# Hash-bucketed attention and a GELU feed-forward on one core: the requests for W_in move to ScalarE's queue, and four orders in the first and last pairs of heads change

## The chip, the core and the metric

The kernel runs on one core of a Trainium2 chip, in one launch. The metric is the device time of one execution in microseconds (us). Of the kernel before, three runs are given; of each kernel one execution was also recorded by the hardware profiler, and the profile and the trace are of that execution.

The names used: PE is TensorE (the matrix engine), DVE is VectorE, ACT is ScalarE, POOL is GpSimd, SP is SyncE, which here does nothing but issue DMAs. SPq and ACTq are the DMA issues in the instruction streams of SP and ACT. PSUM is the memory that the matmuls write.

## The reference, cut to what matters

q, k and v are of shape (4, 8, 768, 64): 4 batches, 8 heads, 768 positions, 64 dimensions, in fp32. `proj` is 64 x 6.

```
q_bits, k_bits = (q @ proj > 0), (k @ proj > 0)          # 6 bits a position
mask   = bucket(q_bits)[:, None] == bucket(k_bits)[None, :]
scores = where(mask, q @ k.T / 8, -1e9)
attn   = softmax(scores) @ v                              # (4, 8, 768, 64)
x      = attn.transpose(0, 2, 1, 3).reshape(3072, 512)
h      = x @ w_in                                         # 512 -> 2048
out    = (h * sigmoid(1.702 * h)) @ w_out                 # 2048 -> 512
```

Every position attends only to the positions in the same hash bucket. `w_in` and `w_out` arrive as 64-bit floats and are turned into 32-bit ones on the chip.

## The kernel before, in words

**Stages.** `attention` (L289 to L736) takes the 32 heads in 16 pairs, n = 0 to 15; the two heads of a pair share the 128 partitions. `feed_forward` follows with a nest of products of halves and quarters (a Strassen-like scheme that needs sums of quarters of x, W_in and W_out). The attention builds x in `xT` (features on partitions, 3072 positions on the free axis) and, pair by pair, turns one 128 x 512 chunk of W_in from 64 to 32 bits.

**One pair.** For each pair n:

- `fetch(n, "k")` and `fetch(n, "q")` (L342, DMAs at L353, four each) and `fetch_v` (L355, DMAs at L365, two) bring the pair's inputs, one to three pairs ahead. `turn` (L414) transposes k and q on DVE into a tile `own` (three in turn; in the profile they also carry the name s_in, whose room one of them uses). `exchange` (L419, four DMAs `s_in<-own` at L424) writes a second copy with the halves of 32 rows swapped.
- `measure` (L426) sums the squares of k or q on ACT into a column of `sizes`; its elementwise output is not used ("junk"). At the end `guard` (L584) takes the largest of the sums, and decides whether a slower, shifted attention must run instead.
- `hashed` (L435) multiplies with `proj` on PE; `featured` (L444) makes the bits into features `f` with one DVE operation (L446), and eight small DMAs (L454) bring f into the tile `feat` of that pair (two in turn). `spread` (L456, two DMAs at L459, then `exchange`) copies the features to further partitions, for pairs from 3 on. A product of features adds 0 to scores of equal buckets and a very large negative number to the others.
- `scores_of_four` (L477) computes four tiles of scores on PE (128 keys x 384 queries of both heads), each with `weigh` (L462): the exponential on ACT (L463). Pairs 0 to 2 use whole rows of 64 (L474), later ones four parts of 32 rows (L491) that run beside each other.
- `values` (L517, matmuls at L524) multiplies the exponentials with v; `unload` (L532) brings the result to `xT` on ACT (L535, L536).
- The denominators: `add_low` (L502 on POOL) and `add_high` (L512, L515 on DVE) add the exponentials over the key tiles, `total` (L538, PE at L546) sums them over the partitions, `invert` (L548, DVE: transpose `rt` at L552, reciprocals at L555 and L559, transpose at L561) inverts, and `norm` (L565, DVE at L567) multiplies `xT` with it. All this happens one or two pairs later.

**The conversion of W_in.** `convert` (L161) is a generator: a DMA brings the raw 512 KB of a chunk (`raw`, L165, one tile), then six DVE operations (L181, L185, L189, L196, L200, L203) and one square on ACT (L193) turn it. `begin(n)` (L576) starts chunk n-2 and issues its DMA; `step(n)` moves a chunk on by one operation. A chunk takes until the beginning of the next pair, where its last operation (L203) frees `raw`.

**PSUM.** Four score tiles s0 to s3 are taken in turn by `in_turn` (L308). The same tiles hold the results of `hashed`, `total` and `values`. A matmul that takes a tile waits until the reader of its last contents is done: the exponential, the unload, the write of f, or the transpose `rt`.

**Sums of x.** `x_sums` (L582) holds four DVE operations on quarters of x (L225 to L228): `x_sums[0]` in pair 14, `x_sums[1]` at the end of pair 14, `x_sums[2]` (L227) in pair 15, `x_sums[3]` (L228) behind the last pair. `in_sums(0)` does the like for W_in on POOL (L217 to L220).

**What sets the order.** The orders of PE, DVE, ACT and POOL are those of the program text (`ORDERED`). SP's order comes from the framework's scheduler. Each DMA is given one of eight completion semaphores in turn, in the scheduler's order over all queues, and so waits for the landing of the DMA eight places before it.

**Around the change, before.** In each pair from 3 on the order is: the write of f for the next pair; `rt` of the pair n-2; the last step of the running chunk; `begin(n)`, which puts the request for the next raw chunk on SP; the feature DMAs on SP; and then the first four tiles of scores. The first chunk, chunk 0, is begun at the end of pair 1. `f` has one buffer. `measure(3, "q")` stands in pair 1, and `fetch(4, "q")` too. `unload(0, 0)` stands behind `featured(1)`, two of whose DMAs go out on ACT's queue. In pair 15 `x_sums[2]` runs on DVE early, and two steps of the last chunk stand ahead of the transpose `rt` of pair 14.

Of the kernel before, what the change touches and what calls it, by code (L numbers as in the profile page):

```python
# [38 lines left out]
def kernel(  # L39
# [249 lines left out]
    def attention(ff):  # L289
# [4 lines left out]
        with actx:  # L294
# [131 lines left out]
            def measure(n, name):  # L426

                x = raws[n, name]
                i = 2 * n + "kq".index(name)
                junk = st.tile([P, S], BF16, tag="junk", name="junk", bufs=1)  # L430
                nc.scalar.activation(junk, x.rearrange("p s i -> p (s i)"), Act.Square, accum_out=sizes[:, i : i + 1])

            dots = {}

            def hashed(n, at):  # L435

                h = dots[n] = at[:, 0:HS]
                for i, x in enumerate("kq"):
                    for c in range(2):
                        r0 = D * i + 32 * c  # L440
                        nc.tensor.matmul(h[r0 : r0 + 32, :], pf[x], xts[n, x][:, c * HS : (c + 1) * HS],
                                         start=True, stop=True)

            def featured(n):  # L444
                f = wk.tile([P, HS], BF16, tag="f", name="f", bufs=1)
                nc.vector.tensor_scalar(f, dots.pop(n), above[:, 0:1], weight[:, 0:1], op0=Alu.is_gt, op1=Alu.mult)  # L446
                yield
                for c in range(2):
                    for i, x in enumerate("kq"):

                        queue = nc.scalar if (n, x, c) == (1, "q", 0) else nc.sync
                        for j in range(2):
                            r0 = D * i + 32 * c + 16 * j
                            queue.dma_start(out=feats[n % 2][x][D * j : D * j + 16, c * HS : (c + 1) * HS], in_=f[r0 : r0 + 16, :])  # L454
# [110 lines left out]
            def norm(n):  # L565
                x, rs = x_of(n), accs.pop(n)
                nc.vector.tensor_tensor(x, x, rs.rearrange("p (t s) -> p t s", t=T), op=Alu.mult)  # L567
# [4 lines left out]
            def step(n, count=1):  # L572
                for _ in range(count):
                    next(conv.get(n, iter(())), None)

            def begin(n):  # L576
                if 0 <= n - 2 < len(in_chunks) - LATE:
                    conv[n] = convert(cv, *in_chunks[n - 2])
                    step(n)


# [29 lines left out]
            measure(1, "q")  # L611
            values(0, 0, high, at[:, 0])
            hashed(1, at[:, 1])
            whole(featured(1))
            unload(0, 0)
            fetch(2, "q")
            fetch_v(1)
            scores(0, 1, high, slots)
# [6 lines left out]
            for n in range(1, last + 1):  # L625

                more = n + 2 <= last
                if n > 1:
                    if n < last:
                        features = featured(n + 1)  # L630
                        next(features)
                    if n > 2:
                        inverse[n - 2] = invert(n - 2)
                        next(inverse[n - 2])
                        step(n - 1)
                        begin(n)
                    if n < last:
                        whole(features)
                scores_of_four(n, ((0, 0), (0, 2)))
                add_high(n - 1, 1, (0, 1))  # L640
                add_low(n, 0)
                if n > 1:
                    next(inverse[n - 2])
                    if more:
                        turn(n + 2, "k")
                    elif n < last:
                        x_sums[0]()
                    else:
                        guard(0)
                        x_sums[2]()  # L650
                add_high(n - 1, 1, (2,))
                if n > 1:
                    norm(n - 2)
                    if more:
                        measure(n + 2, "k")
                    if n + 3 <= last:
                        fetch(n + 3, "k")
                    values(n - 1, 1, every, in_turn()[:, 0])
                    unload(n - 1, 1)
                else:  # L660
                    for x in "kq":
                        turn(2, x)
                    measure(2, "q")
                    for x in "kq":
                        fetch(3, x)
                if n < last:
                    fetch_v(n + 1)
                    if n + 1 >= BY_PARTS:
                        spread(n + 1)
                add_high(n, 0, (0,))  # L670
                step(n, 2)
                scores_of_four(n, ((0, 4), (1, 0)))
                add_low(n, 1, (0,))
                step(n)
                add_high(n, 0, (1,))
                if n > 1 and more:
                    turn(n + 2, "q")
                elif n + 1 == last:
                    x_sums[1]()
                add_high(n, 0, (2,))  # L680
                if more:
                    for x in "kq" if n == 1 else "q":
                        measure(n + 2, x)
                    if n > 1 and n + 3 <= last:
                        fetch(n + 3, "q")
                at = in_turn()
                values(n, 0, every, at[:, 0])
                if n == 1:
                    at1 = in_turn()
                    hashed(2, at[:, 1])  # L690
                    total(0, at1[:, 0])
                if n == last:
                    total(n - 1, at[:, 1])
                unload(n, 0)
                if n == 1:
                    whole(featured(2))
                if n == last:
                    step(n, 2)
                if n in (1, last):
                    inverse[n - 1] = invert(n - 1)  # L700
                    next(inverse[n - 1])
                if n == 1:
                    for x in "kq":
                        turn(3, x)
                        fetch(4, x)
                scores_of_four(n, ((1, 2), (1, 4)))
                add_low(n, 1, (1,))
                if n < last:
                    step(n, 2)
                    at = in_turn()  # L710
                    if more:
                        hashed(n + 2, at[:, 0])
                    if n > 1:
                        total(n - 1, at[:, 1])
                    if n == 1:
                        begin(2)
            next(inverse[last - 1])
            add_high(last, 1, late=True)
            at = place(0)
# [5 lines left out]
            nc.gpsimd.tensor_copy(low_sum[0:1, 0, 0:1], accs_last[0][0:1, 0, 0:1])  # L725
            for f in in_sums(0):
                f()
            norm(last - 1)
            x_sums[3]()
            step(last)  # L730
            inverse = invert(last)
            next(inverse)
# [688 lines left out]
    def whole(steps):  # L1421
        for _ in steps:
            pass
# [49 lines left out]
```

## Time and profile before

| | |
|---|---|
| median of three runs | 865.67 us (864.15 to 866.25) |
| the profiled execution's own time | 865.41 us |
| its span (first to last instruction) | 863.5 us |
| granted clock of TensorE, mean | 0.998 |
| PE, DVE, ACT, POOL busy | 98%, 80%, 39%, 42% of the span |
| pairs 0 and 1, up to 48.09 us | 48.09 us |
| pairs 2 to 15, to 325.23 us | 277.14 us |
| feed-forward, to the end of the span | 538.27 us |

About 1.9 us of the profiled execution's time lie outside its span. How to read the rows: a row of a timeline has the start in us from the span's start, the duration, the engine (SPq and ACTq: a DMA issue), the line of the kernel, the operation, output <- inputs, sizes, a count (xN: N alike in a row, with the time from the first's start to the last's end), and in brackets the idle time of the engine ahead of it and what ended that. A row of a window has its two ends and its length, and then, for PE, the weight loads, DVE, ACT and POOL, the busy time and the number of instructions, and at last the granted clock, the DMA engines' busy share and GB/s. "Pair n" in times means: from PE's first score matmul of that pair to the first of the next one; since the pairs overlap, other pairs' work lies in it too.

### The profile page before, as it was taken

Reading aid. Unit: us, or ns where it says so; the run is one execution under the profiler, and the core shown is the slowest. Engines: PE = TensorE matmul, PEld = TensorE weight load, DVE = VectorE, ACT = ScalarE, POOL = GpSimd, SP = SyncE. Lnnn points to the kernel's source line nnn. Section 1 sums busy time; section 2 is a strip of 40 time slices with the busy share of each in tenths; the row PEclk is TensorE's granted clock in tenths of the full one; section 3 lists DMA queues with packets and bytes.
Section 4 is the critical chain, followed back from the end, with each engine's and each line's share of the span. In section 5 each row is a group of like instructions: output and inputs, shape, how many; then the busy total and the mean of one; then the engine's idle time right before and its main releaser. Section 6 shows DMA issues by size and latency. Waiting matters only on the chain.

```text
span 863.5 us, 15037 instructions
## 1 busy us (share of the span) xinstructions
PE 846.1 (98%) x5631; PEld 524.0 (61%) x5631; DVE 691.7 (80%) x1069; ACT 337.2 (39%) x549; POOL 365.6 (42%) x321
## 2 busy tenths in 40 slices
PE   8999999999999999999999999999999999999996
PEld 4444444444444444566666666644888888888885
DVE  4479788988979995787888888676998977897786
ACT  5666767666656653344444444443000000000000
POOL 4333434333333338999764367568764100000000
PEclk9999999999999999999999999999999999999999
DMA  5648787677767302427465545577854675477534
GB/s 129 104 69 168 147 149 150 130 142 135 130 132 147 84 26 87 158 98 274 165 250 205 202 172 202 212 268 261 277 175 165 201 237 203 155 228 227 194 117 99
DMA packets 165197, 144.04 MB, mean 167 GB/s; under 512 B 124384, under 2 KB 139872, under 8 KB 159872
## 3 DMA queue, kind: packets, MB, share of 16 engines
q1 hardware_dynamic: 156720, 118.76, 50.5%
q10 hardware_dynamic: 8400, 24.28, 8.3%
q8 instruction: 45, 0.74, 0.4%
q14 instruction: 32, 0.26, 0.1%
HBM read 79.69 MB, written 50.33 MB: 151 GB/s over the span
## 4 chain that ended last, share of the span: by engine, by line
PE 80%; DVE 6%; DMA 5%; SPq 3%; issue 2%; ACT 2%; ACTq 0%; DVEq 0%
PE product L1196 29%; PE product L869 22%; PE s L524 9%; PE s L491 7%; PE small L937 6%; PE product L937 3%; DMA raw<-in_moe_w_in_dram 2%; SPq L353 2%; PE s L474 1%; DVE acc L515 1%; ACT e L463 1%; DMA q<-in_q_dram 1%; SPq L454 1%; DVE bits L185 1%; DVE w_in_sb L181 1%
## 5 line engine op out<-in xcount | busy, mean ns | idle before, releaser
L463 ACT ACTIVATE e<-s 128x768 f32<-128x768 f32 x192 | 145.1, 811 | 52.2 <-PE s L491 43.7
L524 PE MATMUL s<-e,v 128*32 128x385 f32 x1536 | 131.1, 488 | 1.0 <-issue 1.0
L502 POOL TENSOR_TENSOR t_x<-e 128x768 f32<-128x768 f32 x32 | 59.3, 1853 | 142.1 <-ACT e L463 117.5
L869 PE MATMUL product<-xT,w_in_sb 128*128 128x512 f32 x216 | 100.0, 593 | 0.1
L524 PEld LDWEIGHTS s<-e,v 128*32 128x32 f32 x1536 | 46.9, 109 | 80.3 <-issue 65.7
L869 PE MATMUL product<-t_x,s_in 128*128 128x512 f32 x192 | 89.4, 592 | 0.0
L491 PE MATMUL s<-s_in 32*128 32x384 f32 x816 | 82.4, 483 | 0.1
L502 POOL TENSOR_TENSOR t_x<-t_x,e 128x768 f32<-128x768 f32 x32 | 55.2, 1726 | 54.2 <-ACT e L463 52.8
L515 DVE TENSOR_TENSOR acc<-acc,e 128x768 f32<-128x768 f32 x63 | 68.6, 1088 | 2.3
L1232 ACT COPY u<-product 128x256 f32<-128x256 f32 x20 | 7.4, 372 | 158.1 <-PE product L1196 124.9
L869 PEld LDWEIGHTS product<-xT,w_in_sb 128*128 128x128 f32 x216 | 40.9, 190 | 35.8 <-issue 32.7
L491 PEld LDWEIGHTS s<-s_in 32*128 32x128 f32 x816 | 42.2, 185 | 21.0 <-issue 1.5
L869 PEld LDWEIGHTS product<-t_x,s_in 128*128 128x128 f32 x192 | 36.5, 190 | 29.7 <-issue 27.0
L491 PE MATMUL s<-own 32*128 32x384 f32 x432 | 46.1, 486 | 0.0
L885 DVE TENSOR_TENSOR u<-product,u 128x256 f32<-128x256 f32 (+1 forms) x60 | 28.4, 486 | 15.9 <-PE product L937 12.8
L491 PE MATMUL s<-feat 32*128 32x384 bf16 x312 | 30.7, 327 | 6.1 <-ACT xT L536 3.2
L491 PEld LDWEIGHTS <-feat 32*128 32x128 bf16 x312 | 9.7, 91 | 42.0 <-issue 28.4
L1196 PE MATMUL product<-raw_g,xT 128*128 128x256 f32 x152 | 35.1, 379 | 0.0
L512 DVE SCALAR_TENSOR_TENSOR acc<-t_x,e 128x768 f32<-128x768 f32 x31 | 29.4, 948 | 5.7 <-ACT e L463 3.6
L226 POOL TENSOR_TENSOR v<-c,v 128x1024 f32<-128x1024 f32 (+1 forms) x15 | 32.4, 2157 | 1.0
L225 POOL TENSOR_TENSOR u<-v,u 128x1024 f32<-128x1024 f32 (+1 forms) x11 | 23.8, 2165 | 21.1 <-ACT v L882 11.9
L885 DVE TENSOR_TENSOR v<-product,v 128x512 f32<-128x512 f32 x24 | 16.5, 689 | 20.2 <-PE product L869 20.2
(298 smaller groups left out, 1813.9 us busy)
## 6 DMA issues: line engine op xcount, KB each, us to landing
raw_g<-g_dram SPq DMA_DIRECT2D x20, 1024.0 KB, 5.1
s_in<-g_dram SPq DMA_DIRECT2D x20, 1024.0 KB, 5.1
g_dram<-c ACTq DMA_DIRECT2D x18, 512.0 KB, 2.9
raw<-in_moe_w_out_dram ACTq DMA_DIRECT2D x16, 512.0 KB, 3.7
raw<-in_moe_w_in_dram SPq DMA_DIRECT2D x15, 512.0 KB, 3.9
s_in<-own SPq DMA_DIRECT2D x36, 192.0 KB, 4.0
v<-in_v_dram SPq DMA_DIRECT2D x32, 192.0 KB, 4.0
k<-in_k_dram SPq DMA_DIRECT2D x60, 96.0 KB, 3.1
```

The costliest lines, as they stand in the source:

```text
L225: return [lambda: eng.tensor_tensor(t1, b12, b11, op=Alu.subtract), lambda: eng.tensor_tensor(b12, b22, b12, op=Alu.subtract), lambda: eng ...
L226: lambda: eng.tensor_tensor(b12, b22, b12, op=Alu.subtract),
L463: nc.scalar.activation(es[c][:, kt, :, 0:HS], ps[:, :, 0:HS], Act.Exp, scale=1.0 / D**0.5)
L491: nc.tensor.matmul(ps[i][:, j, 0:HS], a[r0 : r0 + 32, keys], m[r0 : r0 + 32, cols], start=at == 0, stop=at == 2)
L502: nc.gpsimd.tensor_tensor(low_sum, low_sum if i else e[:, 0], e[:, i + 1], op=Alu.add)
L512: nc.vector.scalar_tensor_tensor(acc, terms[0], T * TINY, terms[1], op0=Alu.add, op1=Alu.add)
L515: nc.vector.tensor_tensor(acc, acc, terms[i + 1], op=Alu.add)
L524: nc.tensor.matmul(av[D * j + d : D * j + d + 32, :], vt[:, t, j, d : d + 32], es[c][:, t, j, :], start=(t == 0), stop=(t == T - 1))
L869: nc.tensor.matmul(ps, wq[LEFT[i]][:, kc, :], xq[RIGHT[i]][:, kc, :], start=(start and kc == 0), stop=(kc == K2 - 1), skip_group_check=not ...
L885: nc.vector.tensor_tensor(dst, x, y, op=Alu.add)
L937: nc.tensor.matmul(x, wq[LEFT[i]], xq[RIGHT[i]], start=start, stop=True, skip_group_check=True)
L1196: nc.tensor.matmul(ps, wq[LEFT[i]][:, c, :], gq[RIGHT[i]][:, c, :], start=(onto is None and c == 0), stop=(c == F4 - 1), skip_group_check= ...
```

## The change

- `measure` writes its unused output as fp32 into the columns of `xT` that belong to the last pair of heads (which are written with x later), in place of a bf16 tile of its own.
- `f` has two buffers in place of one.
- `begin` passes ACT's queue to `convert`: the raw chunk's DMA (L165) is issued by ACT. `begin(n)` stands behind the pair's first four tiles of scores, and so behind their four exponentials on ACT, in place of the start of the pair. For n = 2 it stands in pair 2 in place of the end of pair 1. It is 14 DMAs in all, one in each of the pairs 2 to 15. SP keeps 24 of 25 DMAs a pair.
- In pair 0 `unload(0, 0)` stands ahead of `featured(1)` and its two DMAs on ACT's queue.
- `measure(3, "q")` and `fetch(4, "q")` move from pair 1 into pair 2, behind its first exponentials.
- In pair 15 `x_sums[2]` moves behind the attention, beside `x_sums[3]`, after POOL's sums of W_in and ahead of `norm` of pair 14. The two steps of the last chunk stand behind `rt` of pair 14 in place of ahead of it.

The orders of PE and POOL stay as they were. In the changed program the raw chunk on ACT waits, in the steady pairs, for the landing of the third of the eight feature DMAs of the same pair (eight places before it) and for L203 of the chunk before.

```diff
--- before.py
+++ after.py
@@ -427,8 +427,8 @@
 
                 x = raws[n, name]
                 i = 2 * n + "kq".index(name)
-                junk = st.tile([P, S], BF16, tag="junk", name="junk", bufs=1)
-                nc.scalar.activation(junk, x.rearrange("p s i -> p (s i)"), Act.Square, accum_out=sizes[:, i : i + 1])
+                junk = xT[:, HP - 1, (B - 1) * S : B * S].rearrange("p (s i) -> p s i", i=32)
+                nc.scalar.activation(junk, x, Act.Square, accum_out=sizes[:, i : i + 1])
 
             dots = {}
 
@@ -442,7 +442,7 @@
                                          start=True, stop=True)
 
             def featured(n):
-                f = wk.tile([P, HS], BF16, tag="f", name="f", bufs=1)
+                f = wk.tile([P, HS], BF16, tag="f", name="f", bufs=2)
                 nc.vector.tensor_scalar(f, dots.pop(n), above[:, 0:1], weight[:, 0:1], op0=Alu.is_gt, op1=Alu.mult)
                 yield
                 for c in range(2):
@@ -575,7 +575,7 @@
 
             def begin(n):
                 if 0 <= n - 2 < len(in_chunks) - LATE:
-                    conv[n] = convert(cv, *in_chunks[n - 2])
+                    conv[n] = convert(cv, *in_chunks[n - 2], nc.scalar)
                     step(n)
 
 
@@ -611,8 +611,8 @@
             measure(1, "q")
             values(0, 0, high, at[:, 0])
             hashed(1, at[:, 1])
+            unload(0, 0)
             whole(featured(1))
-            unload(0, 0)
             fetch(2, "q")
             fetch_v(1)
             scores(0, 1, high, slots)
@@ -633,10 +633,13 @@
                         inverse[n - 2] = invert(n - 2)
                         next(inverse[n - 2])
                         step(n - 1)
-                        begin(n)
                     if n < last:
                         whole(features)
                 scores_of_four(n, ((0, 0), (0, 2)))
+                if n == 2:
+                    measure(3, "q")
+                    fetch(4, "q")
+                begin(n)
                 add_high(n - 1, 1, (0, 1))
                 add_low(n, 0)
                 if n > 1:
@@ -647,7 +650,6 @@
                         x_sums[0]()
                     else:
                         guard(0)
-                        x_sums[2]()
                 add_high(n - 1, 1, (2,))
                 if n > 1:
                     norm(n - 2)
@@ -679,8 +681,7 @@
                     x_sums[1]()
                 add_high(n, 0, (2,))
                 if more:
-                    for x in "kq" if n == 1 else "q":
-                        measure(n + 2, x)
+                    measure(n + 2, "k" if n == 1 else "q")
                     if n > 1 and n + 3 <= last:
                         fetch(n + 3, "q")
                 at = in_turn()
@@ -694,15 +695,15 @@
                 unload(n, 0)
                 if n == 1:
                     whole(featured(2))
-                if n == last:
-                    step(n, 2)
                 if n in (1, last):
                     inverse[n - 1] = invert(n - 1)
                     next(inverse[n - 1])
+                if n == last:
+                    step(n, 2)
                 if n == 1:
                     for x in "kq":
                         turn(3, x)
-                        fetch(4, x)
+                    fetch(4, "k")
                 scores_of_four(n, ((1, 2), (1, 4)))
                 add_low(n, 1, (1,))
                 if n < last:
@@ -712,8 +713,6 @@
                         hashed(n + 2, at[:, 0])
                     if n > 1:
                         total(n - 1, at[:, 1])
-                    if n == 1:
-                        begin(2)
             next(inverse[last - 1])
             add_high(last, 1, late=True)
             at = place(0)
@@ -725,8 +724,9 @@
             nc.gpsimd.tensor_copy(low_sum[0:1, 0, 0:1], accs_last[0][0:1, 0, 0:1])
             for f in in_sums(0):
                 f()
+            for f in x_sums[2:]:
+                f()
             norm(last - 1)
-            x_sums[3]()
             step(last)
             inverse = invert(last)
             next(inverse)
```

## The prediction

> **What bounds the kernel now.** I read the page first, then busy time by pair of heads, then the orders of SP, DVE, PE and ACT in one slow and one fast pair, and last the chain that ended last.
>
> ```profile
> span 863.5 us, 15037 instructions
> PE 846.1 (98%) x5631; PEld 524.0 (61%) x5631; DVE 691.7 (80%) x1069; ACT 337.2 (39%) x549; POOL 365.6 (42%) x321
> ...
> raw<-in_moe_w_in_dram SPq DMA_DIRECT2D x15, 512.0 KB, 3.9
> ```
>
> TensorE carries the span and the edits take no matmul away, so only its stalls can be won. They are found by stage. I cut the span where PE begins each pair's first scores; a window runs from one pair's first matmul to the next pair's (length, then busy time of each engine). Below, pair 3 begins at 69.31, pair 4 at 89.28, pair 5 at 107.80, pair 7 at 145.25, pairs 8 to 13 at 163.78 to 262.78, pair 15 at 299.92.
>
> ```profile
> 69.31:89.28 19.97, 19.86 (x237) 8.97 (x234) 16.50 (x23) 12.59 (x21) 6.46 (x4) 1.00 0.85 160
> 89.28:107.80 18.52, 18.52 (x238) 8.26 (x235) 15.55 (x23) 12.61 (x22) 7.27 (x4) 1.00 0.73 141
> 107.80:126.74 18.94, 18.94 (x237) 8.80 (x234) 15.54 (x23) 12.61 (x22) 6.84 (x4) 1.00 0.80 155
> 145.25:163.78 18.53, 18.53 (x238) 8.28 (x235) 17.48 (x23) 12.61 (x22) 7.09 (x4) 1.00 0.67 130
> 163.78:183.09 19.31, 19.01 (x237) 8.40 (x234) 17.51 (x23) 12.73 (x22) 7.20 (x4) 1.00 0.69 127
> 183.09:203.37 20.28, 19.17 (x236) 8.40 (x233) 17.76 (x24) 12.65 (x22) 7.65 (x4) 1.00 0.68 129
> 203.37:223.81 20.44, 19.18 (x236) 8.40 (x232) 17.85 (x24) 12.65 (x22) 7.38 (x4) 1.00 0.80 146
> 223.81:242.92 19.11, 18.85 (x237) 8.29 (x234) 17.30 (x25) 12.63 (x22) 7.44 (x4) 1.00 0.86 158
> 242.92:262.78 19.86, 18.84 (x236) 8.38 (x233) 16.59 (x22) 12.66 (x22) 7.35 (x5) 1.00 0.67 126
> 262.78:281.89 19.11, 18.85 (x237) 8.29 (x234) 18.25 (x25) 12.60 (x22) 7.55 (x4) 1.00 0.67 143
> ...
> 299.92:325.23 25.31, 23.46 (x285) 10.45 (x282) 23.37 (x34) 12.12 (x19) 8.82 (x7) 1.00 0.08 22
> ```
>
> The same work takes 18.52 us in pair 4, where PE never stops, 18.53 in pair 7, and 19.11 to 20.44 in pairs 8 to 13. Over 18.52 these six lose 0.79, 1.76, 1.92, 0.59, 1.34 and 0.59, together **6.99 us**. That is the largest sum to win. The clock column is 1.00 throughout, so none of it is clock.
>
> Why they lose is seen in the order of SP's DMAs. The raw chunk of W_in is asked for 1.90 us after the start of pair 4, and 8.54 us after the start of pair 9:
>
> ```profile
> 91.18 0.35 SPq L165 DMA_DIRECT2D raw<-in_moe_w_in_dram  x1
> ...
> 151.41 0.53 SPq L165 DMA_DIRECT2D raw<-in_moe_w_in_dram  x1
> ...
> 189.74 1.80 SPq L454 DMA_DIRECT2D feat<-f  x3
> 191.63 0.54 SPq L165 DMA_DIRECT2D raw<-in_moe_w_in_dram  x1
> 192.22 3.31 SPq L454 DMA_DIRECT2D feat<-f  x5
> 198.21 1.18 SPq L459 DMA_DIRECT2D feat<-feat  x2
> ```
>
> It lands 3.9 us later (the page's median), and DVE wants it early. The next rows are DVE's: L181 on time in pair 4, the spare idle at the start of pair 7, then L181 and the steps behind it late in pair 9; the last is PE's stall from that.
>
> ```profile
> 98.73 0.68 DVE L181 SCALAR_TENSOR_TENSOR w_in_sb<-raw,mask_3fffffff 128x512 uint32<-128x512 uint32 x1
> ...
> 145.39 0.68 DVE L446 TENSOR_SCALAR f<-s,above,weight 128x384 bf16<-128x384 f32 x1 [2.65 <-PE s L546]
> ...
> 195.49 0.69 DVE L181 SCALAR_TENSOR_TENSOR w_in_sb<-raw,mask_3fffffff 128x512 uint32<-128x512 uint32 x1 [2.20 <-DMA raw<-in_moe_w_in_dram]
> 196.22 1.92 DVE L185 SCALAR_TENSOR_TENSOR bits<-raw,w_in_sb 128x512 uint32<-128x512 uint32 x1
> ...
> 201.38 2.17 DVE L196 SCALAR_TENSOR_TENSOR w_in_sb<-raw,w_in_sb 128x512 f32<-128x512 uint32 x1
> ```
>
> ```profile
> 200.38 0.34 PE L491 MATMUL s<-feat 32*128 32x384 bf16 x2 [0.86 <-ACT xT L536]
> ```
>
> In pair 4 L181 starts 9.45 us after the pair's start and the pair loses nothing; in pair 9 it starts 12.40 after it, having waited 2.20, and two steps of L181's size, which takes 0.68, take 1.92 and 2.17. DVE's spare 2.65 us is spent, ACT's unload behind L193 is late, and PE waits for the released PSUM tile.
>
> **The change part by part.** *The chunk on ScalarE.* The issue now stands behind the pair's first four exponentials. ACT in the fast pair 7:
>
> ```profile
> 147.02 2.94 ACT L463 ACTIVATE e<-s 128x768 f32<-128x768 f32 x4 [1.55 <-PE s L491]
> ...
> 152.43 0.16 ACT L535 COPY vs<-s 128x1 f32<-128x1 f32 x1 [1.65 <-PE s L524]
> ```
>
> The exponentials end at 149.96, 4.7 us into the pair; plus 3.9 the chunk lands at +8.6, before the +9.45 at which DVE can first use it. That is 0.85 early. Some 0.6 more would be free: in pair 7 raw was asked for at +6.16, landed 3.9 later at about +10.06, and the pair took 18.53. The issue itself is not in this trace at this place; the nearest ACT rows (below) are two issues in 1.46, 0.73 each, SP's take 0.35 to 0.54. I take 0.5, and it lies in the 1.65 us that ACT idles before the unload; without that cover it would delay the unload by at most 0.73 per pair. So the 6.99 goes, and with it pair 5's 0.42, where SP's round was also late. What is late next in those pairs is PE itself: 18.52 is its bare time.
>
> The new ACT order adds a wait: the program gives its DMAs eight completion semaphores in turn, so each DMA waits for the landing of the one eight places before it, and in the steady pairs that is the third of the eight feature DMAs of the same pair on SP. In the chain a feature DMA without raw ahead of it lands in 1.79:
>
> ```profile
> 49.32 1.79 DMA feat<-f
> ...
> 67.52 3.92 DMA s_in<-own
> ```
>
> The features start when f is written, 0.82 us into pair 7 (145.39 and 0.68); the third is issued two places of 0.6 later and lands near +3.9, ahead of +4.7. This holds only if SP keeps up. In before SP's round was too long: raw slipped from +1.90 in pair 4 to +6.16 in pair 7, 1.4 us a pair over 18.52, near 20.0. It loses one issue (0.53 and a gap, 0.6). Features asked for behind raw on SP also land behind it, which kept the spread (L459) waiting:
>
> ```profile
> SPq L459 <- DMA feat<-f: 15.6, 11, 2.8
> ```
>
> That is 1.4 a time, which should halve. 20.0 less 0.6, less 0.7, less some of the queue in which raw's half megabyte stood gives 17.5 to 18.7: about the pair's own time. I take no drift. The Trainium skill speaks against this: "DMA: Bandwidth & Descriptors", section "Issuing engines are not separate DMA queues", says that DMAs of all issuing engines run on the same 16 engines and interleave, so that another issuer saves only sequencer time. By that alone the drift would go on at 0.8 a pair. The trace speaks for more: the wait for the features is measured behind raw on the same queue, and no run here has yet shown two queues side by side in this stage.
>
> *Pairs 0 to 3.* Rows of ACT's queue, PE, ACT and DVE:
>
> ```profile
> 25.35 1.46 ACTq L454 DMA_DIRECT2D feat<-f  x2
> ```
>
> ```profile
> 28.07 4.09 PE L524 MATMUL s<-e,v 128*32 128x385 f32 x48 [1.02 <-issue]
> ...
> 52.26 0.34 PE L474 MATMUL s<-feat 64*128 64x384 bf16 x2 [1.05 <-DVE f L446]
> ```
>
> ```profile
> 42.56 0.84 ACT L431 ACTIVATE junk<-q 128x768 bf16<-128x768 f32 x1 [1.75 <-DMA q<-in_q_dram]
> ```
>
> ```profile
> 44.27 0.68 DVE L446 TENSOR_SCALAR f<-s,above,weight 128x384 bf16<-128x384 f32 x1 [1.84 <-ACT xT L536]
> ```
>
> unload(0,0) stood behind two issues of 1.46; now it comes first, and PE's 1.02 at 28.07 goes. The second f tile takes the 1.05 at 52.26. But neither reaches the end of pair 3: there PE waits for the exchange that lands at 71.44 (67.52 and 3.92, above), the end of an unbroken row of SP issues that begins when f of pair 2 is written. That f waited 1.84 for an unload that stood behind measure(3,"q"), itself 1.75 late for q. With the measurement moved to pair 2 and PE 1.02 earlier, f comes near 42.6 instead of 44.27, SP's row as much earlier. So pairs 0 to 3 win about **1.8**, not 2.1 plus 1.7; between 0 (if another DMA in the row takes its place) and 3.1 (1.02 and 1.05 and 1.0 more). In pair 4 the eighth feature DMA now waits for chunk 1 on ACT: 0 to 1.0 lost, I take **0.1**. A measurement's output in f32 in place of bf16 costs nothing that I can see: 0.84 above, beside 0.74 for an exponential of that size with f32 out.
>
> *The last pair.* DVE, then PE:
>
> ```profile
> 306.98 2.08 DVE L227 TENSOR_TENSOR t_x<-xT,t_x 128x1024 f32<-128x1024 f32 x1
> ...
> 318.13 0.58 DVE L552 STREAM_TRANSPOSE rt<-s 128x384 f32<-128x384 f32 x1
> ...
> 334.64 0.69 DVE L885 TENSOR_TENSOR c<-product,c 128x512 f32<-128x512 f32 x1 [1.10 <-ACT c L1074]
> ```
>
> ```profile
> 318.76 0.34 PE L491 MATMUL s<-feat 32*128 32x384 bf16 x2 [1.35 <-DVE rt L552]
> ```
>
> The 2.08 leaves the pair and rt moves ahead of two conversion steps of 0.69, so PE's stall at 318.76 goes (1.35 named, about 1.7 with refilling). The last sums of the denominator on DVE then end the pair, so I take **1.5**. The 2.08 returns behind the attention, on DVE, beside the first products of the feed-forward; DVE idles 1.10 there before 334.64, and PE works ahead of it. With that cover gone it costs up to 2.08; I take 0.
>
> **Sum.** 6.99 + 0.42 + 1.8 - 0.1 + 1.5 = 10.6. The profiled execution took 865.41, its span is 863.5; 865.41 - 10.6 = **854.8**, and the median of the runs before, 865.67, lies 0.3 above the profiled one.
>
> **The rivals.**
> *SP still slips, slowly.* With a round 0.3 over the pair, the slack of raw (0.8 until ACT waits, 0.85 until DVE waits, 0.6 free) is gone after some seven pairs, and pairs 10 to 13 lose again what they lost, 4.4: 859.2. For it: the estimate of the round straddles the pair. Chance 0.14.
> *The chunk is not what the slow pairs pay for*, but DVE's load beside POOL: then only 0.42 + 1.8 - 0.1 + 1.5 is won, 861.8. Against it: pair 4 has the same instructions without loss. 0.05.
> *No change.* Half of the pairs win, the other half lose to the wait on ACT: within 2.6 of 865.4. 0.04.
> *Slower: ACT is held at the issue.* If SP's round loses only the issue, 0.6 of the 1.4, it stays 0.8 too long, and the third feature DMA reaches the phase of pair 9 (the first at 189.74, +6.65, the third 1.2 later and landed 1.8 after that, near +9.6). ACT's unload, at +7.18 in pair 7 with a measurement of 0.84 ahead of it, stays in place only if the issue comes by about +5.8, and PE has some 1.3 more before its turn of tiles reaches that one. Held longer, ACT keeps its measurement, unload and exponentials behind the issue, and the chunk lands at +13.5, 1.1 later than before. Pair 9 lost 1.76 for a wait of 2.20 of which 0.6 is free, 1.1 a us; six pairs lose 1.2 more each, 7.3, against the other gains of 3.6: 869.1. It decides where the features start later than some 4 us into a pair; in pair 7 of before they did (three of 0.6 ahead of 151.41: +4.3). 0.10. It is the outcome that the Trainium skill's rule above, in "DMA: Bandwidth & Descriptors", would lead to.
>
> **How the numbers follow.** Forecast 0.67, its own range 853 to 857 (pairs 0 to 3 and the last pair at their bounds). The range for 8 in 10 adds the first two rivals and leaves out no change, slower and the best end: 852.0 to 861.8. A measurement of this kernel tells about 0.3%, 2.6 us, from nothing. Faster by more: 0.67 + 0.14 + 0.05 = 0.86; within it 0.04; slower 0.10.
>
> **What would show it.** Right: pairs 8 to 13 at 18.5 to 18.7; raw issued on ACT near +4.7 in all of them; no wait of L181 for raw; no 1.02 at PE's values(0,1); pair 3's stall ending near 69.6; pair 15 near 23.8. Wrong: ACT's idle before L535 ending on a late issue (slower); SP's features starting later from pair to pair (slip); PE waiting for sums of x in the first products of the feed-forward (tail).

## The result

| | before | after |
|---|---|---|
| median | 864.91 us (4 runs) | 876.04 us (4 runs, 875.73 to 879.67) |
| ratio | | 1.0139, 95% interval 1.0106 to 1.0172: slower |
| profiled execution, span | 863.5 us | 873.9 us |

Forecast were 854.8 us and a range of 852.0 to 861.8. The change is 1.4% slower. One execution of e3 (872.72 us) and one of e8 (874.55 us), below, fell in the slower state of the chip and are left out of their ratios.

In the profiled executions the 10.4 us lie here: pairs 0 to 3 are 0.85 shorter (pair 3 ends at 88.43 in place of 89.28), pairs 4 to 13 are 10.99 longer (pairs 4 to 7 6.1 of it, pair 5 alone 3.6; pairs 8 to 13 4.9), pair 14 is equal, pair 15 is 0.74 shorter, and the feed-forward is 1.0 longer.

Some of the windows of after, cut by pair as before: pairs 4, 5, 8, 11 and 12, then 15, then the feed-forward (length, busy PE, PEld, DVE, ACT, POOL, granted clock, DMA share, GB/s). A pair in which PE never waits takes 18.52; such a pair is called bare.

```profile
88.43:107.77 19.34, 18.89 (x236) 8.71 (x233) 17.00 (x22) 12.63 (x22) 7.08 (x4) 1.00 0.55 115
107.77:130.32 22.55, 20.85 (x237) 9.20 (x234) 18.43 (x24) 12.56 (x22) 7.09 (x4) 1.00 0.83 150
...
169.01:189.56 20.55, 18.86 (x238) 8.38 (x235) 17.40 (x23) 12.59 (x22) 7.71 (x5) 1.00 0.77 134
...
230.52:253.61 23.09, 20.79 (x236) 8.77 (x233) 16.18 (x24) 12.57 (x22) 7.67 (x5) 0.93 0.81 143
253.61:272.13 18.52, 18.52 (x236) 8.26 (x234) 16.50 (x23) 12.61 (x22) 6.89 (x4) 1.00 0.72 136
...
310.06:334.63 24.57, 23.93 (x285) 10.45 (x282) 21.99 (x33) 11.96 (x19) 9.28 (x7) 1.00 0.07 23
334.63:873.90 539.27, 531.81 (x2011) 381.55 (x2010) 424.63 (x699) 131.82 (x213) 245.18 (x199) 1.00 0.56 193
```

Of the pairs 4 to 13 only pair 12 has the bare 18.52. The waits of after say which wait is new (engine, line, released by: us in total, times, longest):

```profile
ACT xT L431 <- DMA feat<-f: 32.2, 10, 4.8
DVE w_in_sb L181 <- DMA raw<-in_moe_w_in_dram: 20.7, 10, 3.8
PE s L491 <- ACT xT L536: 10.0, 9, 2.3
```

```profile
SPq L459 <- DMA feat<-f: 24.8, 10, 3.5
```

The third row is the one that costs PE time: 10.0 us, after 3.2 in before. L431 is the measurement behind the request on ACT; it does not read features. What waits is the request ahead of it, for its completion semaphore; this wait is called the hold. In each of the pairs 4 to 13 the trace has the request go out 0.08 us after the landing of the feature DMA that had the same semaphore before it: the fourth of the eight in pair 4, the fifth in pair 5, the third in pairs 6 to 13. L181's wait for raw has doubled from 10.3 us to 20.7, and SP's wait ahead of the spread, which should have halved, has grown from 15.6 to 24.8. Pair 8 (start 169.01), in order of SP, ACT, DVE, PE; from here on +4.7 means 4.7 us after the start of the pair:

```profile
167.68 3.57 SPq L353 DMA_DIRECT2D q<-in_q_dram  x3
171.29 2.40 SPq L424 DMA_DIRECT2D s_in<-own  x2
173.79 4.96 SPq L454 DMA_DIRECT2D feat<-f  x8
```

```profile
170.78 2.94 ACT L463 ACTIVATE e<-s 128x768 f32<-128x768 f32 x4 [1.55 <-PE s L491]
177.43 0.33 ACTq L165 DMA_DIRECT2D raw<-in_moe_w_in_dram  x1
177.88 0.84 ACT L431 ACTIVATE xT<-k 128x768 f32<-128x768 f32 x1 [4.17 <-DMA feat<-f]
...
178.73 0.14 ACT L535 COPY vs<-s 128x1 f32<-128x1 f32 x1
```

```profile
169.15 0.68 DVE L446 TENSOR_SCALAR f<-s,above,weight 128x384 bf16<-128x384 f32 x1 [1.21 <-PE s L546]
181.23 0.69 DVE L181 SCALAR_TENSOR_TENSOR w_in_sb<-raw,mask_3fffffff 128x512 uint32<-128x512 uint32 x1 [2.69 <-DMA raw<-in_moe_w_in_dram]
```

```profile
179.53 0.34 PE L491 MATMUL s<-feat 32*128 32x384 bf16 x2 [1.69 <-ACT xT L536]
```

f is there at 169.83, but SP is still busy with q and the exchange and issues the first feature DMA at 173.79. ACT is done with its exponentials at 173.72 (+4.7, as forecast), is held, and issues the request at 177.43 (+8.4). The unload comes at 178.73, 9.7 into the pair in place of 7.2 in pair 7 of before, PE stalls for 1.69, and the chunk reaches DVE at 181.23, 12.2 into the pair. PE stalls at this place, +9.6 to +11.4, in pairs 7 to 11 and 13.

Pair 5, the second longest, loses most of its time in another way. In pair 4 the features start with f (+0.84), and the request goes out in their midst, at 94.72. The feature DMA that SP had asked for 0.06 us earlier takes 5.51 us to land, where the one ahead of it took 1.77. The spread waits for it, the exchange behind the spread lands late, and PE waits for that exchange in pair 5 (first the chain that ended last, then PE):

```profile
94.66 5.51 DMA feat<-f
...
105.58 4.55 DMA s_in<-s_in
```

```profile
110.17 1.36 PE L491 MATMUL s<-s_in 32*128 32x384 f32 x5 [0.78 <-DMA s_in<-s_in]
```

The first products with v start 5.46 us into pair 5; in pair 9 of e5 (below), where nothing waits ahead of them, 3.02. So some 2.4 of the 4.0 us that pair 5 takes over the bare time are lost there.

### The profile page after: what moved, and what is told of

Its sections match the earlier page's. It is cut to its first block, busy times and chain, and to the rows that moved or that the text cites. A ratio compares the mean times of both kernels' runs of the same rounds, so it can differ in the third digit from the quotient of the medians.

```text
span 873.9 us, 14972 instructions
## 1 busy us (share of the span) xinstructions
PE 851.7 (97%) x5631; PEld 524.7 (60%) x5631; DVE 692.5 (79%) x1069; ACT 335.9 (38%) x549; POOL 367.8 (42%) x321
## 4 chain that ended last, share of the span: by engine, by line
PE 67%; DVE 9%; DMA 8%; POOL 6%; SPq 4%; issue 3%; ACT 2%; ACTq 0%; DVEq 0%; POOLq 0%
PE product L1196 29%; PE product L869 16%; PE s L524 7%; PE small L937 5%; PE s L491 5%; DVE acc L515 3%; PE product L937 2%; PE s L474 2%; DMA feat<-f 2%; SPq L353 2%; DMA raw<-in_moe_w_in_dram 2%; SPq L454 1%; DMA q<-in_q_dram 1%; ACT e L463 1%; DMA k<-in_k_dram 1%
## 5 line engine op out<-in xcount | busy, mean ns | idle before, releaser
L491 PE MATMUL s<-s_in 32*128 32x384 f32 x816 | 85.6, 488 | 1.6 <-DMA s_in<-own 0.8
L515 DVE TENSOR_TENSOR acc<-acc,e 128x768 f32<-128x768 f32 x63 | 73.6, 1169 | 2.3
L885 DVE TENSOR_TENSOR u<-product,u 128x256 f32<-128x256 f32 (+1 forms) x60 | 28.4, 485 | 15.6 <-PE product L937 12.8
L491 PEld LDWEIGHTS <-feat 32*128 32x128 bf16 x312 | 10.4, 91 | 49.1 <-issue 37.0
```

The source lines that it names most:

```text
L491: nc.tensor.matmul(ps[i][:, j, 0:HS], a[r0 : r0 + 32, keys], m[r0 : r0 + 32, cols], start=at == 0, stop=at == 2)
L515: nc.vector.tensor_tensor(acc, acc, terms[i + 1], op=Alu.add)
L885: nc.vector.tensor_tensor(dst, x, y, op=Alu.add)
```

## The experiments

**Theory A**: ACT is held at the request by the semaphore that a feature DMA on SP releases. **B**: the chunk's transfer delays the features and the spread on whichever queue it is asked for, so SP's row is no shorter. **C**: the other edits lose. **D** (later): only the late chunk costs, not the hold. Ratios are to the kernel before, run beside, with 95% intervals. SP's row means its DMA issues for one pair, in their order. Each run's rows have the line numbers of its own kernel, so that L454 here is L456, L459 or L460 there.

**e1_rest_only**: the other edits without the request's move.

```diff
-                    conv[n] = convert(cv, *in_chunks[n - 2], nc.scalar)
+                    conv[n] = convert(cv, *in_chunks[n - 2])
...
                         step(n - 1)
+                        begin(n)
...
                 scores_of_four(n, ((0, 0), (0, 2)))
...
-                begin(n)
...
                         total(n - 1, at[:, 1])
+                    if n == 1:
+                        begin(2)
```

> The changed kernel with begin as it was before (request on SP at the head of the pair, chunk 0 at the end of pair 1); all other edits kept. Theory A (ACT is held at the request by the semaphore that a feature DMA of the same pair releases) and theory B (the request's half megabyte delays the features and the spread wherever it is issued, so SP's round is no shorter): 861 to 865 us, a gain of 0 to 4 from the first and the last pairs, and pairs 8 to 13 as slow as before. Theory C (the loss comes from the other edits): 870 or more.

1.0008 (0.9991 to 1.0024), 865.9 us, 0.9 above the range of A and B and far below C's.

**e2_request_only**: before, with the request's move and nothing else.

```diff
-                    conv[n] = convert(cv, *in_chunks[n - 2])
+                    conv[n] = convert(cv, *in_chunks[n - 2], nc.scalar)
...
                         step(n - 1)
-                        begin(n)
...
                 scores_of_four(n, ((0, 0), (0, 2)))
+                if n > 1:
+                    begin(n)
...
-                    if n == 1:
-                        begin(2)
```

> The kernel before with only the request moved to ACT behind the first four exponentials. A and B: 874 to 880 us, the whole loss. C: 863 to 867.

1.016 (1.0133 to 1.0187), 878.6 us. The move alone is the whole loss; C falls. The other edits win a little in the first and last pairs and lose part of it again; in time e1 is not told apart from before. In the profile of e1, pairs 0 to 3 are 0.95 shorter (pair 3 ends at 88.33), and the last pair and the feed-forward read:

```profile
298.20:322.54 24.34, 23.93 (x285) 10.47 (x282) 21.78 (x32) 11.96 (x19) 9.76 (x7) 1.00 0.07 23
322.54:861.80 539.26, 531.80 (x2011) 381.54 (x2010) 424.72 (x699) 131.73 (x213) 245.00 (x199) 1.00 0.57 193
```

Pair 15 wins 0.97, the feed-forward pays 0.99 back.

**e3_pool_queue**: the change with the request on POOL's queue.

```diff
-                    conv[n] = convert(cv, *in_chunks[n - 2], nc.scalar)
+                    conv[n] = convert(cv, *in_chunks[n - 2], nc.gpsimd)
```

> The changed kernel with the request on POOL's queue at the same place of the program. POOL has semaphores of its own for its DMAs, so the request waits for no feature DMA, and ACT issues nothing. A: no hold on ACT, the chunk lands before DVE wants it, 855 to 861 us. B: the transfer still delays the features, SP stays late, 866 to 874 us.

1.0016 (0.9986 to 1.0045), but the executions behind this fall into two groups: 857.9 and 859.7, as by A, and five from 867.0 to 870.1, as by B. The profile is of the fastest, at 857.86; windows of pairs 9 and 13, and POOL and SP in pair 9:

```profile
182.32:200.84 18.52, 18.52 (x237) 8.29 (x234) 15.55 (x23) 12.62 (x22) 7.86 (x5) 1.00 0.76 137
...
256.39:274.91 18.52, 18.52 (x237) 8.27 (x235) 16.42 (x23) 12.62 (x22) 7.79 (x5) 1.00 0.76 152
```

```profile
184.49 0.57 POOL L165 DMA_DIRECT2D raw<-in_moe_w_in_dram  x1 [2.24 <-DVE w_in_sb L203]
```

```profile
186.18 6.00 SPq L454 DMA_DIRECT2D feat<-f  x8
```

In this execution every pair from 4 to 13 but pair 5 (18.65) takes 18.52, although SP's features still start 3.9 us into the pair. That speaks for A, with two limits: POOL asks for the chunk 2.2 us into the pair, where ACT in after asks at +6.0 or later, and what the five executions near 867 to 870 did differently isn't in a trace.

**e4_no_request**: the change with one chunk loaded once and converted 14 times; most of W_in is left out.

```diff
+            kept = cv.tile([P, CW, 2], U32, tag="raw", name="raw")
+            nc.scalar.dma_start(out=kept, in_=in_chunks[0][1])
...
-                    conv[n] = convert(cv, *in_chunks[n - 2], nc.scalar)
+                    conv[n] = convert(cv, *in_chunks[n - 2], nc.scalar, raw=kept)
```

> The changed kernel without 13 of the 14 requests: one chunk of W_in is loaded ahead of the pairs and converted 14 times (most of W_in is left out; the square goes to a free part of t_x so that the chunk stays). A and B: pairs 4 to 13 at 18.5 us each, 853 to 857. If the chunk is not what the pairs pay for: 862 or more. SP's row per pair shows what the request costs the other DMAs: by B the features start within 1 us of f, by A alone they start as late as in the changed kernel.

0.9926 (0.9902 to 0.995), 859.1 us; 18.52 in the pairs 4 to 13 but pair 5 (19.07). The time lies above the forecast mostly because the pairs 0 to 3 end at 91.01, 2.6 later than in after. And SP's row slips even without the chunk. Pairs 4 and 13, and the features in them:

```profile
91.01:109.53 18.52, 18.52 (x238) 8.27 (x235) 15.55 (x23) 12.61 (x22) 7.28 (x4) 1.00 0.65 112
258.23:276.75 18.52, 18.52 (x237) 8.30 (x234) 16.42 (x23) 12.63 (x22) 7.24 (x4) 1.00 0.58 111
```

```profile
91.85 4.45 SPq L456 DMA_DIRECT2D feat<-f  x6
...
262.84 3.27 SPq L456 DMA_DIRECT2D feat<-f  x5
```

They start 0.84 into pair 4 and 4.61 into pair 13: with 24 DMAs and no request at all the row is on average 0.4 us longer than a pair. In e3's profiled execution, with the chunk on POOL's queue, it is the same (0.84 and 4.68). My picture of a row that fits the pair without raw was false; and B is not the whole of it either.

**e5_short_hold**: two rooms (buffers) for raw chunks, the request one pair ahead. The core of the edit; e6 to e8, e10 and e12 share the rooms and also drop `begin(n)` at this place:

```diff
+            rooms2 = [t_x[:, 1].rearrange("p k f -> p (k f)").bitcast(U32).rearrange("p (c two) -> p c two", two=2),
+                      cv.tile([P, CW, 2], U32, tag="raw", name="raw")]
...
-                    conv[n] = convert(cv, *in_chunks[n - 2], nc.scalar)
+                    conv[n] = convert(cv, *in_chunks[n - 2], nc.scalar, raw=rooms2[n % 2])
...
                 scores_of_four(n, ((0, 0), (0, 2)))
-                begin(n)
+                if n > 1:
+                    begin(n + 1)
```

> The changed kernel with two rooms for raw chunks (the second in t_x[:, 1], which lies idle until the sums of x), and the request on ACT at the same place but for the next pair's chunk, so that DVE never waits for it. The request now stands behind the landing of the first, not the third, feature DMA. Theory A (ACT held by that semaphore): the hold is there but some 1.3 us shorter, the request at +5 to +6.8, the unload at +6.5 to +8.2, inside what PE can bear; 857 to 863 us, no L181 wait for raw. Theory D (what costs is only that the chunk comes late to DVE, not the hold): 856 to 858, all pairs 4 to 13 at 18.5.

1.0141 (1.0124 to 1.0158), 877.4 us, about as long as the change and outside both forecasts. My label is wrong: from pair 6 on the request waited for the third feature as before, so the hold was not shorter. But DVE no longer waits for the chunk. Pair 9 of e5, ACT, DVE, PE:

```profile
201.72 0.36 ACTq L167 DMA_DIRECT2D t_x<-in_moe_w_in_dram  x1
202.20 0.85 ACT L436 ACTIVATE xT<-k 128x768 f32<-128x768 f32 x1 [4.11 <-DMA feat<-f]
```

```profile
202.84 0.68 DVE L186 SCALAR_TENSOR_TENSOR w_in_sb<-raw,mask_3fffffff 128x512 uint32<-128x512 uint32 x1
```

```profile
203.85 0.34 PE L496 MATMUL s<-feat 32*128 32x384 bf16 x2 [1.63 <-ACT xT L541]
```

The pair starts at 193.39: DVE begins the chunk at +9.45, on time, ACT's issue is at +8.3, and the pair takes 20.48. In pairs 7 to 13 together e5 takes 11.4 over the bare time, after 13.0 and before 7.0: the hold without a late chunk costs most of what hold and late chunk cost, and D falls. The equal totals say less, because 3.6 of e5's loss against before lies ahead of pair 4, and 4.1 in pair 5, where PE again waits for an exchange.

**e6_sp_two_rooms**: the rooms, but the request on SP at the head of the pair, for the next one.

```diff
-                    conv[n] = convert(cv, *in_chunks[n - 2], nc.scalar)
+                    conv[n] = convert(cv, *in_chunks[n - 2], raw=rooms2[n % 2])
...
                     if n < last:
+                        begin(n + 1)
                         whole(features)
```

> Two rooms as above, but the request stays on SP at the head of the pair, one pair ahead. A and D: neither hold nor late chunk, pairs 4 to 13 at 18.5 to 18.6, 856 to 859 us. If SP's row is too long for the pair by itself (B), the exchange comes late to PE in the later pairs: stalls behind s_in<-own, 862 or more.

0.9942 (0.9923 to 0.9962), 860.7 us: 0.6% faster than before, and between the two forecasts, which hold in turn: pairs 4 to 9 take 18.52, and of the later ones most are slow because SP's row has slipped.

```profile
182.96:201.48 18.52, 18.52 (x237) 8.28 (x234) 15.55 (x23) 12.65 (x22) 7.32 (x4) 1.00 0.69 133
...
239.78:259.27 19.49, 18.86 (x237) 8.64 (x235) 16.12 (x23) 12.63 (x22) 6.57 (x4) 1.00 0.78 143
```

```profile
230.99 1.80 SPq L459 DMA_DIRECT2D feat<-f  x3
...
237.48 1.61 SPq L464 DMA_DIRECT2D feat<-feat  x2
```

```profile
240.76 0.33 PE L496 MATMUL s<-feat 32*128 32x384 bf16 x1 [0.63 <-DMA feat<-feat]
```

The features start 10.6 us into the pair that begins at 220.38, the spread follows at 237.48, and PE waits for it at the head of the next pair. So in these pairs SP's lateness reaches PE directly only when the features start some 8 to 11 us into a pair (7.8 in e10, below, 10.6 here); through ACT's semaphore it did so at 3 to 5. (Pair 5 of after is the exception: there the features start early, but land late.)

**e7_act_pair_end** and **e12_act_behind_unload**: the rooms, with the request on ACT behind the pair's last exponentials (first place below, e7), or behind `unload(n, 0)` (second, e12), where other DMAs stand eight places ahead.

```diff
                 scores_of_four(n, ((1, 2), (1, 4)))
+                if n > 1:
+                    begin(n + 1)
```

```diff
                 unload(n, 0)
+                if n > 1:
+                    begin(n + 1)
```

> Two rooms, the request on ACT behind the pair's last four exponentials, where it stands behind the landing of an exchange DMA some 4 us old. A: ACT is held little or not, and idle there anyway; 855 to 859 us. If any request on ACT costs what the change cost, 868 or more.

> Two rooms, the request for the next pair's chunk on ACT behind the unload of the pair's first values (some 15 us into the pair). The DMA eight places before it is now one of the k loads, which SP issues 7 us behind the first feature DMA and which is landed by +8 to +14 as long as SP's row keeps the phase that it has without the request (features at +0.8 to +4.7). If the semaphore's phase is all that made the request on ACT dear: no hold, no late chunk, pairs 4 to 13 at 18.5, 856 to 859 us, faster than the change and the kernel before. If SP's row slips further than that, ACT is held there too and the later pairs lose: 862 or more.

1.0131 (1.0113 to 1.0148), 876.4 us, and 1.0214 (1.0189 to 1.0238), 884.4 us. The gains that I hoped for came in neither: there, too, ACT was held, by an exchange and by a k load of SP's row. First e7, then e12:

```profile
199.32 2.92 ACT L468 ACTIVATE e<-s 128x768 f32<-128x768 f32 x4 [4.12 <-DMA s_in<-own]
```

```profile
175.96 2.92 ACT L468 ACTIVATE e<-s 128x768 f32<-128x768 f32 x4 [3.35 <-DMA k<-in_k_dram]
```

But the hold is not all of their loss. In both, 9.5 us of it lie in pair 3 alone, and in e7 pairs 4 to 13 are together only 1.25 longer than in before. Pair 3 of e7, and the chain ahead of it:

```profile
70.15:99.65 29.50, 25.01 (x236) 11.23 (x233) 17.10 (x24) 13.11 (x22) 6.90 (x5) 0.83 0.63 131
```

```profile
68.83 5.33 DMA raw<-in_moe_w_in_dram
...
74.18 2.59 DMA s_in<-own
```

Here the semaphore works the other way round: SP's third exchange DMA was given the semaphore of the chunk that ACT had just asked for, and went out only when the chunk had landed, 5.33 us after its request; PE waited 3.67 for the exchange; then the granted clock fell too (0.83 in the pair). In e12 it was the second exchange DMA, and the chunk took 5.93 us to land.

**e8_pool_two_rooms**: e6 with the request on POOL's queue.

```diff
-                    conv[n] = convert(cv, *in_chunks[n - 2], raw=rooms2[n % 2])
+                    conv[n] = convert(cv, *in_chunks[n - 2], nc.gpsimd, raw=rooms2[n % 2])
```

> Two rooms, the request on POOL's queue at the head of the pair, one pair ahead. The one-room version on POOL's queue ran between 858 and 873 us, and its profiled execution at 857.9 had every pair at 18.5. If its slow executions come from chunks that land late, they go here: 856 to 859 in all executions. If they come from something else that POOL's queue does, the spread stays, to 870.

1.0064 (1.0037 to 1.0091); one execution at 860.5 and four from 867.6 to 872.1 us. The spread stays though the chunk has a pair's time to land, so it doesn't come from late chunks. Its cause stays open.

**e9_short_row**: the change, with SP's row cut short: v is loaded for pairs 0 to 3 only and q for pairs 0 to 4, so that most of q and v is left out.

```diff
+                if name == "q" and n > 4:
+                    raws[n, name] = raws[4, name]
+                    return
...
+                if n > 3:
+                    vts[n] = vts[n - 2]
+                    return
```

> The changed kernel with a shorter row on SP: v is loaded for the pairs 0 to 3 only and q for 0 to 4 (later pairs use the same ones again, so most of q and v is left out), 18 DMAs a pair instead of 24. The request stays on ACT, with one room, and its semaphore still is that of an early feature DMA of the same pair. If the changed kernel lost because SP's row is longer than a pair, and ACT inherits its lateness through the semaphore: features start with f, the third lands by +4, the request goes out at +4.7, pairs 5 to 13 at 18.5; 854 to 858 us. If ACT's wait or the chunk's way over ACT's queue costs something by itself: 865 or more.

0.9908 (0.9892 to 0.9925), 857.2 us. Pair 9 (start 181.03), its window, SP and ACT:

```profile
181.03:199.54 18.51, 18.51 (x236) 8.25 (x232) 15.54 (x23) 12.73 (x22) 7.27 (x4) 1.00 0.46 105
```

```profile
181.87 5.17 SPq L460 DMA_DIRECT2D feat<-f  x8
```

```profile
186.22 0.33 ACTq L165 DMA_DIRECT2D raw<-in_moe_w_in_dram  x1
186.68 0.84 ACT L437 ACTIVATE xT<-k 128x768 f32<-128x768 f32 x1 [0.95 <-DMA feat<-f]
```

Same request, same place, and in pairs 4 to 13 the semaphore of the third feature DMA: with a row that fits, the features start 0.84 into the pair, the request is out at +5.2 (at +3.8 to +4.2 in the other nine pairs), and the pairs from 4 to 13 are bare. Taking the row's lateness away takes the loss away, which shows that a request on ACT is not dear by itself, but by SP's lateness. The edit takes away six issues a pair and their transfers together, so it does not say which of the two makes the row too long.

**e10_sp_behind_features**: e6 with the request behind the features on SP. **e11_rooms_alone**: before with e6's edit and nothing else.

```diff
                     if n < last:
-                        begin(n + 1)
                         whole(features)
...
                     unload(n - 1, 1)
+                    begin(n + 1)
```

> The two rooms with the request on SP, but behind the eight features in place of ahead of them, where SP waits for their landing anyway. If the slip of SP's row (features 2 us later from pair to pair in the version ahead of them) came from features that land behind the chunk, the row is some 2 us shorter and the later pairs keep 18.5: 856 to 859 us. If the sum of the transfers sets the row, the slip stays: 859 to 863.

> The kernel before with nothing but the two rooms and the request one pair ahead, on SP at its old place. If the edits to the first and last pairs are worth the 1.7 us of span that they showed alone: 861 to 864 us. If they are worth nothing in time: 858.7 to 862, as with them.

0.9968 (0.9956 to 0.9981), 862.0 us, and 0.9956 (0.9942 to 0.997), 861.5 us. The slip stays: in e10 the features start 1.6 into pair 4 and 8.5 into pair 13, in e11 2.4 and 9.6, some 0.8 a pair in both; in e10 pairs 4 to 6 lose, too. In time the three are not told apart. The rooms carry the gain of e6, the change's other edits nothing that shows.

## Why the prediction was wrong, point by point

- **The failed step** is "I take no drift", with the row of 17.5 to 18.7 behind it. Even without the request SP's row is about 0.4 longer than a pair, 18.9 (e4), and in after the features start 2.0 to 4.8 us into the pair from pair 5 on. Two terms of the sum were off. The 20.0 was read from the slip of raw, 1.4 a pair; but between pairs 4 and 7 raw had moved behind three feature DMAs of its pair. The features themselves slip 0.8 a pair with the request on SP (e11), which is a row of 19.3. And taking the request off SP saved 0.4 of that (e3's profiled execution and e4), where 1.3 and more were taken off. The forecast said of the third feature's landing that it "holds only if SP keeps up"; SP didn't, and e9, where it does, comes within 2.4 us of the forecast (857.2) and shows its picture.
- **The issue at +4.7** was taken for the earliest. In e9 it is out at +3.8, while the last of the four exponentials still runs.
- **The wait that the change adds** was named, with its DMA and its semaphore, and what stands behind it on ACT. That is the rival "ACT is held at the issue", given a chance of 0.10 and 869.1 us. Its mechanism is what happened; its price was too low by 6.9 against the measured median. About half of that are the other gains, put at 3.6: measured are 0.85 and 0.74, less 1.0. The other half is the pairs: the rival had pairs 8 to 13 lose 7.3, and they lost 4.9, but pairs 4 to 7, which it left out, lost 6.1. Pairs 7 to 11 and 13 stall by the hold itself, where I had priced the late chunk (e5 shows the hold without it). Pair 4 (18.52 became 19.34) still pays for the late chunk, at its second unload; pair 5 (18.94 became 22.55) mostly for the late exchange, which no rival had.
- **6.99 from pairs 8 to 13**: the term is real. With the chunk early and no hold they are bare (e3's profiled execution, e4, e9), or nearly (e6).
- **The spread's wait**, which "should halve", grew to 24.8 us. The chunk on another queue does hold up features on SP's: 5.51 us in place of 1.77 in pair 4 of after. The Trainium skill, "DMA: Bandwidth & Descriptors", section "Issuing engines are not separate DMA queues", would have SP save only its issue time; here the trace agrees (0.4 a pair saved, an issue of 0.53), and I had given the wait for features behind raw more weight than it could bear.
- **Pairs 0 to 3**, 1.8: measured 0.85 to 0.95, half. PE's 1.02 and 1.05 went and were swallowed by the exchange, as said, but pair 3 itself grew from 19.97 to 21.71 in after.
- **Pair 15**, 1.5: measured 0.74 to 0.97. **The tail at 0** was wrong: the feed-forward is 1.0 longer in after and e1. PE has a stall there of 0.77 for ACT's L991, some 70 us behind the moved sum, that before has not. How the moved sum leads to it wasn't tried.
- **Slow slip and "not the chunk"** as rivals: the slip is there, but most of the price runs over ACT and not over DVE. The second falls with e4, whose pairs are bare without the chunk.

## What to carry to other kernels

Before a DMA moves to a compute engine's queue, ask what that engine waits for to issue it: if completion semaphores are given in turn over all queues, the engine inherits the lateness of the DMA that had the semaphore last. A queue that only issues can be late for free as long as what it brings still comes in time; the trace of before showed its lateness growing from pair 5 to pair 9, and that was the number to bound the new wait with. A second buffer, with the request one round earlier on the queue where it was, bought 4.4 us (e6), some two fifths of the 10.6 that I had forecast for the whole change.

## What the runs showed of the hardware

A PE stall can cost more than its length. In pair 11 of after, rows of PE:

```profile
230.69 1.46 PE L491 MATMUL s<-s_in 32*128 32x384 f32 x16
...
241.95 0.34 PE L491 MATMUL s<-feat 32*128 32x384 bf16 x2 [2.30 <-ACT xT L536]
241.96 2.52 PE L491 MATMUL s<-s_in 32*128 32x384 f32 x16
244.41 4.83 PE L524 MATMUL s<-e,v 128*32 128x385 f32 x48
249.17 0.34 PE L491 MATMUL s<-feat 32*128 32x384 bf16 x4
249.34 1.46 PE L491 MATMUL s<-s_in 32*128 32x384 f32 x16
```

Behind the stall of 2.30 the same 16 matmuls take 2.52 in place of 1.46 and the 48 of the values 4.83 in place of 4.09 (1.46 again at 249.34, and 4.09 in pair 12), and the pair's window has a granted clock of 0.93. The granted clock was 0.50 from 242.54 to 245.95 and 1.00 elsewhere in the pair; in the 3.41 us ahead of the drop PE was busy for 1.11. Behind the stalls of 1.69 in pair 8 and of 2.22 in pair 10 the clock stayed at 1.00. The Trainium skill, "TensorE: Matmul & The Clock Gate", section "Why this matters for your kernels", warns of idle gaps over about 3 us; here 2.30 was enough, and the measurement decides. The length alone does not: in e12 the clock fell to 0.50 behind a stall of 2.03 (at 177.44) and not behind one of 2.29 (at 199.34). What else decides was not tried.
